# Dividing the attention weights on ScalarE ahead of VectorE's transpose, with the values matmul five steps behind

## The chip, the core and the metric

The kernel runs on one core of a Trainium2 chip. A core has five engines, each with its own in-order instruction queue: TensorE (PE in the profile; PEld is its weight load), VectorE (DVE), ScalarE (ACT), GpSimd (POOL) and SyncE (SP), which here issues nearly all DMAs. The metric is the device time of one execution in microseconds; lower is better.

## The reference, cut to what matters

Eight batches of eight heads, 576 rows of 64 numbers each, all fp32. Each row of scores keeps its 32 largest, is turned into weights by exponentials and a division by their sum, and multiplies V; the heads side by side make `x` (4608 by 512), which goes through two matrix multiplications with `h - tanh(h)` between.

```python
scores = scale * np.matmul(q, k.transpose(0, 1, 3, 2))
kth = np.partition(scores, -top_k, axis=-1)[..., -top_k:-top_k + 1]     # top_k = 32
scores = np.where(scores >= kth, scores, -1000000000.0)
attn = np.exp(scores - np.max(scores, axis=-1, keepdims=True))
attn = attn / (np.sum(attn, axis=-1, keepdims=True) + 1e-09)
x = np.matmul(attn, v)                    # then (B,H,S,D) -> (B*S, H*D)
h = x @ w_in                              # 512 -> 2048
out = (h - np.tanh(h)) @ w_out            # 2048 -> 512
```

## The kernel before

**Steps.** The attention is cut into 144 steps. A step is one batch, one pair of heads (`hp`) and one tile of 128 query rows; the two heads of the pair are the index `t`. Batch 0 has 18 steps of one kind (`pe` steps, whose weights TensorE transposes); the other seven batches have 18 steps each, 126 together, whose weights VectorE transposes. Two steps of the same head pair and adjacent query tiles form a pair (`nq = 2`, `i = 0, 1`); the 64 rows left over from two head pairs form a single step (`rem`). Each batch after the first has eight pairs and two such singles.

**What one step does, engine by engine.** `scores` multiplies Q and K on PE into one PSUM tile `scps` (there is only one) and ACT copies it to `sc` (L246). `search` on DVE reads both (L268, L269: min and max of the two halves), then finds the 32 largest in four rounds of MAX8 (L276) and MATCH_REPLACE8 (L279). `mask` makes a threshold on POOL (`tb`, L295), a relu on ACT (L308, one instruction per head), a subtraction on POOL (L311) and a check on POOL (`bad`, L315), which reads the search's work tile `ab` (two of these exist). `expo` takes exponentials on ACT with their sums (L331) and POOL adds a small number to the sums (`rd`, L341). `invert` takes the reciprocal on DVE, once for a pair (L346). `turn_z` transposes the weights in 32 by 32 blocks on DVE into `zx` (L377); there are two `zx` places. `spread_keys` sends `zx` to DRAM (`there`, L390) and back in another order (`et`, L392, four DMAs); there is one `et` place for pairs and one, `et_rem`, for singles. `values` multiplies V with `et` on PE (L436) into `av`.

**Division before.** The weights stay undivided. `spread` copies the reciprocals out to 64 columns on POOL (`rx`, L356), PE transposes that (L444) beside `av`, ACT copies both to `xs` (L448), and POOL multiplies the two into `xT` (L460; L451 for singles).

**The feed-forward part.** Each finished unit of 128 or 256 rows of `x` puts its items into a work list: H items (`ffn_h`, L489, PE; after every second one ACT takes `tanh` and a copy, L501 and L502, and POOL subtracts, L503) and O items (`ffn_o`, L510, PE; after eight of them ACT copies the result, L520, and SP stores it). H and O results share two PSUM tiles.

**Order.** The order of every engine's queue is the order in which the Python loop emits. Iteration `n` emits: `values` of the step that is `lag` behind; `mask(n - 1)`; `search(n)`, in whose round 0 the function `between` puts `invert(n - 2)` and `turn_z(n - 2)`; `spread_keys(n - 2)` if that step closes a pair; then feed-forward items, `scores(n + 1)`, items, `expo(n - 1)`, items, and the loads of K, Q and V rows. `deal` takes the items from the list at a rate that `rate` sets so that the list lasts until the next unit is due. `lag` is 2 for `pe` steps and 4 for the others. V rows of a head pair are loaded one iteration before its first step.

Of the kernel before, what the change touches and what calls it, by code (L numbers as in the profile page):

```python
# [17 lines left out]
TOP = 32  # L18
EPS = 1.0e-9
J = 4  # L20


class Step:
# [4 lines left out]
    def __init__(self, b, hp, qt, unit, col, i=0, nq=1, pe=False):  # L28
        self.b, self.hp, self.qt, self.unit, self.col = b, hp, qt, unit, col
        self.i, self.nq, self.pe = i, nq, pe  # L30
        self.rem = qt == J
        self.last = i == nq - 1

        self.lag = 2 if pe else 4


class Unit:
# [11 lines left out]
def kernel(  # L49
# [9 lines left out]
    nc = tc.nc  # L59
# [10 lines left out]
    G = 32  # L70
    NG = P // G
    KC = 2 * S // P
    G = 32
    NG = P // G
    WJ = 4
    FJ = CF // WJ
    scale = 1.0 / float(D) ** 0.5
# [5 lines left out]
    def pool(name, bufs, **kw):  # L83
        return ctx.enter_context(tc.tile_pool(name=name, bufs=bufs, **kw))
# [5 lines left out]
    abpool = pool("ab", 2)  # L90
    mpool = pool("m", 3)
    zpool = pool("z", 2)
    etpool = pool("et", 1)
    xpool = pool("x", 2)
    xrpool = pool("xr", 1)
    thpool = pool("th", 4)
# [16 lines left out]

    spare = consts.tile([P, 4, NW, 2], U32, name="spare")
    later = spare[:].rearrange("p a n w -> p (a n w)").bitcast(FP32)
    zx2 = [consts.tile([P, 4 * S], FP32, name="zx")[:], later[:, 0 : 4 * S]]
    et_rem = later[:, 4 * S : 6 * S]
    e1151 = consts.tile([P, 1], FP32, name="e1151")
    nc.gpsimd.memset(e1151[:], 1151.0 * 2.0**23)
# [5 lines left out]

    first = zx2[0][:, 0 : 4 * NW].bitcast(U32).rearrange("p (a n w) -> p a n w", a=2, w=2)
    slots = [(spare[:, i], spare[:, 2 + i], 8 * CD) for i in range(2)]
    slots.append((first[:, 0], first[:, 1], 8 * CD))  # L130
    for j in reversed(range(WJ)):
# [52 lines left out]
    def half(t):  # L184
        return slice(t * D, (t + 1) * D)
# [155 lines left out]
        nc.gpsimd.tensor_scalar(rd[:, g.i, :], den[:], EPS, None, ALU.add)  # L341

    def invert(n):
        if steps[n].last:
            rd = rds[n][:, 0 : steps[n].nq, :]
            nc.vector.reciprocal(rd, rd)  # L346

    rxs = {}

# [7 lines left out]
                rx[:, 0:nq], rd[:, 0:nq].unsqueeze(3).to_broadcast([P, nq, 2, D])  # L357
            )

    zxs, ets, last_zx = {}, {}, [0]  # L360

    def group(a):
        return slice(a * G, (a + 1) * G)
# [6 lines left out]
    def turn_z(n):  # L370


        g, z = steps[n], st.pop(n)["z"]
        if g.i == 0:
            last_zx[0] ^= 1
        zx = zxs[n] = zxs.pop(n - 1) if g.i else zx2[last_zx[0]]
        nc.vector.transpose(  # L377
            tiles(zx, g.nq)[:, :, :, g.i, :].rearrange("p c k j -> p k c j"),
            z[:].rearrange("p (k c j) -> p k c j", c=NG, j=G),
        )  # L380

    def spread_keys(n):


        zx = zxs.pop(n)
        rem = steps[n].rem
        et = ets[n] = et_rem if rem else etpool.tile([P, 4 * S], FP32, tag="et", name="et")
        w = steps[n].nq * S // 2
        there = dpool.tile([P, NG * w], FP32, tag=f"there{steps[n].nq}", name="there")
        nc.sync.dma_start(there[:], zx[:, 0 : NG * w])  # L390
        for c in range(NG):
            nc.sync.dma_start(  # L392
                et[group(c), 0 : NG * w].rearrange("i (a x) -> i a x", a=NG),
                there[:, c * w : (c + 1) * w].rearrange("(a i) x -> i a x", a=NG),
            )

    def turn_pe(n):

        g, z = steps[n], st.pop(n)["z"]
        if g.rem:  # L400
            et = et_rem
        elif g.i:
            et = ets.pop(n - 1)
        else:
            et = etpool.tile([P, 4 * S], FP32, tag="et", name="et")[:]
        ets[n] = et
        et = tiles(et, g.nq)[:, :, :, g.i, :].rearrange("p a k j -> p k a j")
        for k0 in range(0, KC, J):
            kn = min(J, KC - k0)
            zt = zt_ps.tile([P, 512], FP32, tag="zt", name="zt")  # L410
            for k in range(kn):
                nc.tensor.transpose(  # L412
                    zt[:, k * P : (k + 1) * P], z[:, (k0 + k) * P : (k0 + k + 1) * P], ident[:]
                )
            nc.scalar.copy(  # L415
                et[:, k0 : k0 + kn],
                zt[:, 0 : kn * P].rearrange("p (k a j) -> p k a j", a=NG, j=G),
            )
            if k0:
                yield  # L420

    def values(n):

        g = steps[n]
        nq, u = g.nq, g.unit
        et = tiles(ets.pop(n), nq)
        rx = rxs.pop(n)
        w = nq * P
        av = zt_ps.tile([P, 2, N], FP32, tag="zt", name="av")
        for i in range(2 if g.rem else 1):  # L430
            cols = half(i) if g.rem else slice(0, w)
            es = et[:, 2 * i : 2 * i + 2] if g.rem else et
            hp = g.hp + i
            for c in range(J + 1):
                for t in range(2):
                    nc.tensor.matmul(  # L436
                        av[half(t), 0, cols],
                        vb[g.b, hp][:, t, c, :] if c < J else vr[g.b, hp][:, t, :],
                        es[:, :, (J + 1) * t + c if c < J else J].rearrange("p a i j -> p a (i j)"),
                        start=(c == 0),  # L440
                        stop=(c == J),
                    )
        for i in range(nq):
            nc.tensor.transpose(  # L444
                av[:, 1, 0:w].rearrange("p (a i j) -> p i a j", a=NG, i=nq)[:, i], rx[:, i].rearrange("p t d -> p (t d)"), ident[:]
            )
        xs = xrpool.tile([P, 2, N], FP32, tag="xs", name="xs")
        nc.scalar.copy(xs[:, :, 0:w], av[:, :, 0:w])  # L448
        if g.rem:
            for i in range(2):  # L450
                nc.gpsimd.tensor_tensor(  # L451
                    xt(u)[:, g.hp + i, g.col : g.col + R],
                    xs[:, 0, half(i)],
                    xs[:, 1, half(i)],
                    ALU.mult,
                )
        else:

            xv = xs[:, :, 0:w].rearrange("p s (a i j) -> p s i a j", a=NG, i=nq)
            nc.gpsimd.tensor_tensor(  # L460
                xt(u)[:, g.hp, g.col : g.col + w].rearrange("p (i a j) -> p i a j", a=NG, i=nq),
                xv[:, 0],
                xv[:, 1],
                ALU.mult,
            )
        if n in done:
            work.extend(ffn(u))

# [104 lines left out]
    def run(exact):  # L573
# [4 lines left out]
        def at(n, fn):  # L578
            todo.setdefault(n, []).append(fn)
# [3 lines left out]
        for i, (b, hp) in enumerate(pairs):  # L583
            n = next(n for n, g in enumerate(steps) if (g.b, g.hp) == (b, hp))
            for x, name in enumerate("kq"):
                m = max(n - 5 + x, turned.get(name, -4))
                if b == 0 and not exact:
                    m = -4
                at(m, lambda x=(name, b, hp, exact): load_rows(*x))
                if x and i < NHP and not exact:  # L590
                    at(-4, lambda: load_piece())
                turn = lambda x=(name, b, hp): turn_rows(*x)
                if 0 < i < NHP:
                    at_round.setdefault((n - 1, 0), []).append(turn)
                    turned[name] = n - 1
                else:
                    at(n - 3 + x, turn)
                    turned[name] = n - 3 + x
            at(n - 1, lambda b=b, hp=hp: load_v(b, hp))

# [41 lines left out]
        def between(i):  # L644
            for fn in at_round.pop((n, i), []):
                fn()
            if i == 0 and here(-2):
                invert(n - 2)
                if not steps[n - 2].pe:
                    turn_z(n - 2)  # L650


        ready, begun = {}, {}
# [13 lines left out]
        def rate():  # L667


            have, low, high = len(work), 0.0, None  # L670
            coming = sorted((t, u.n // 8) for u, t in ready.items() if t > n)
            for t, k in coming + [(NS + 4, 0)]:
                r = have / max(t - n, 1)
                high = r if high is None else min(high, r)
                have += k
            for u, t in begun.items():
                if t > n and u in before:
                    need = [i + 1 for i, x in enumerate(work) if x[1] is before[u]]
                    if need:
                        low = max(low, need[-1] / (t - n))  # L680
            return max(low, high)
# [8 lines left out]
                credit -= 1  # L690
            credit = min(credit, 1.0)

        for n in range(-4, NS + 4):
            pe = here(-2) and steps[n - 2].pe
            if here(-3) and not steps[n - 3].pe:
                spread(n - 3)
            for m in (n - 4, n - 3):
                if 0 <= m < NS and steps[m].last and steps[m].lag == n - m:
                    values(m)
            share, usable = rate(), converted[0]  # L700
# [5 lines left out]
            if here(0):  # L706
                search(n, exact, between)
            elif here(-2):
                between(0)
            if here(-2) and not pe and steps[n - 2].last:  # L710
                spread_keys(n - 2)
            if pe:
# [63 lines left out]
```

## Time and profile before

| | |
|---|---|
| time, median of 3 runs | 1538.54 us (1538.29 to 1539.8) |
| the profiled execution | 1541.86 us, of which the span of the profile is 1540.1 us |
| PE | 1441.5 us busy, 94% of the span |
| DVE | 1346.9 us busy, 87% |
| POOL | 940.9 us busy, 61% |
| ACT | 883.4 us busy, 57% |
| granted TensorE clock over the span | 0.981 |

A row of groups reads: line, engine, operation, output<-input by the program's names, shapes, count, then busy time in us, mean ns of one instruction, and the engine's idle time just ahead of them with what ended it. A row of the timeline reads: start in us, length in us, engine, line, operation, and in brackets the idle time ahead of it and its releaser. The profile shows two matmul instructions for each fp32 multiplication of the program, and one for a transpose.

### The profile page before, as it was taken

How to read it: one execution, taken by the hardware profiler on the slowest of the kernel's cores; microseconds unless marked ns; L12 is line 12 of the kernel's file. 1: busy time of each engine (PE TensorE's matmuls, PEld its weight loads, DVE VectorE, ACT ScalarE, POOL GpSimd, SP SyncE). 2: the span in 40 equal slices, each digit the busy share in tenths (PEclk: the TensorE clock that was granted, in tenths of full speed). 3: DMA queues.
4: the chain of work that ended last, by engine and by line, in shares of the span. 5: the costliest groups of instructions: out<-in, count | busy, mean ns of one | idle time of the engine just before them, and what ended most of it. 6: DMA issues, size and time to landing. Idle time of an engine off the chain costs nothing.

```text
span 1540.1 us, 24174 instructions
## 1 busy us (share of the span) xinstructions
PE 1441.5 (94%) x7428; PEld 911.6 (59%) x7428; DVE 1346.9 (87%) x3828; ACT 883.4 (57%) x1567; POOL 940.9 (61%) x1525
## 2 busy tenths in 40 slices
PE   2567898999999999999999999999999999999997
PEld 1355566556566665656566665656566665656673
DVE  6988899999999999999999999999999999997300
ACT  4887776556555565556565565656565565655320
POOL 2777677567575675757575675757575675746420
PEclk9887999999999999999999999999999999999999
DMA  9944114546754575446655565456655566534400
GB/s 233 367 168 172 50 32 102 143 130 176 173 157 137 146 168 161 127 141 154 177 136 146 146 161 160 128 149 154 172 136 149 146 153 165 147 114 116 137 7 16
DMA packets 255466, 221.61 MB, mean 144 GB/s; under 512 B 197728, under 2 KB 204896, under 8 KB 248160
## 3 DMA queue, kind: packets, MB, share of 16 engines
q1 hardware_dynamic: 253552, 219.75, 53.1%
q8 instruction: 61, 1.00, 0.3%
q14 instruction: 77, 0.63, 0.2%
q10 hardware_dynamic: 1776, 0.22, 0.1%
HBM read 136.17 MB, written 83.76 MB: 143 GB/s over the span
## 4 chain that ended last, share of the span: by engine, by line
PE 79%; DVE 7%; ACT 4%; DMA 3%; issue 2%; SPq 2%; POOL 2%; DVEq 0%; ACTq 0%; POOLq 0%
PE hps L489 30%; PE ops L510 29%; PE av L436 10%; PE scps L238 9%; DVE m L276 2%; DVE ab L279 2%; PE av L444 2%; SPq L201 1%; DMA et<-there 1%; ACT z L308 1%; ACT f L159 1%; PE zt L412 1%; DMA zx<-in_moe_w_in_dram 1%; DVE ab L268 1%; DVE ab L271 1%
## 5 line engine op out<-in xcount | busy, mean ns | idle before, releaser
L510 PE MATMUL ops<-w_out,g 128*128 128x512 f32 x1152 | 520.5, 598 | 0.0
L489 PE MATMUL hps<-xT,w_in 128*128 128x256 f32 (+1 forms) x2176 | 471.4, 372 | 1.2 <-POOL xT L460 1.2
L276 DVE MAX8 m<-ab 128x8 f32<-128x288 f32 (+1 forms) x1152 | 464.1, 444 | 0.0
L311 POOL TENSOR_TENSOR z<-sc,z 128x576 f32<-128x576 f32 x288 | 400.2, 1412 | 77.1 <-ACT z L308 77.1
L489 PEld LDWEIGHTS hps<-xT,w_in 128*128 128x128 f32 x2176 | 390.7, 193 | 73.9 <-issue 20.7
L279 DVE MATCH_REPLACE8 ab<-m,ab 128x288 f32<-128x288 f32 x864 | 376.0, 443 | 0.0
L510 PEld LDWEIGHTS ops<-w_out,g 128*128 128x128 f32 x1152 | 211.4, 191 | 244.7 <-issue 240.7
L308 ACT ACTIVATE z<-sc,tb 128x576 f32<-128x576 f32 x288 | 207.6, 769 | 153.8 <-POOL tb L295 153.8
L503 POOL TENSOR_TENSOR g<-g,th 128x512 f32<-128x512 f32 x144 | 183.8, 1276 | 123.5 <-ACT g L502 109.0
L331 ACT ACTIVATE z<-z,nb 128x576 f32<-128x576 f32 x288 | 221.6, 773 | 8.7 <-POOL z L311 8.6
L246 ACT COPY sc<-scps 128x1152 f32<-128x1152 f32 x144 | 160.8, 1116 | 108.5 <-PE scps L238 106.4
L238 PE MATMUL scps<-kT,qT 64*128 64x288 f32 (+1 forms) x1280 | 188.1, 445 | 30.2 <-DVE qT L223 27.7
L238 PEld LDWEIGHTS scps<-kT,qT 64*128 64x128 f32 (+1 forms) x1280 | 101.4, 184 | 118.9 <-issue 56.4
L436 PE MATMUL av<-et,vb 128*64 128x256 f32 (+1 forms) x1088 | 133.3, 381 | 38.4 <-ACT et L415 30.6
L268 DVE TENSOR_TENSOR ab<-scps,sc 128x576 f32<-128x576 f32 x144 | 107.6, 747 | 68.0 <-POOL bad L315 55.0
L460 POOL TENSOR_TENSOR xT<-xs 128x256 f32<-128x256 f32 (+1 forms) x68 | 47.2, 695 | 168.0 <-ACT xs L448 168.0
L501 ACT ACTIVATE th<-hps 128x512 f32<-128x512 f32 x144 | 85.4, 593 | 106.8 <-PE hps L489 104.4
L448 ACT COPY xs<-av 128x512 f32<-128x512 f32 (+1 forms) x84 | 44.1, 525 | 169.6 <-PE av L444 169.6
L436 PEld LDWEIGHTS av<-et,vb 128*64 128x64 f32 x1088 | 75.2, 140 | 101.0 <-issue 36.3
L341 POOL TENSOR_SCALAR rd<-den 128x2 f32<-128x2 f32 x144 | 33.4, 232 | 139.4 <-ACT z L331 90.9
L271 DVE MAX8 ab<-ab 128x8 f32<-128x288 f32 x288 | 116.5, 446 | 0.0
L269 DVE TENSOR_TENSOR ab<-scps,sc 128x576 f32<-128x576 f32 x144 | 107.5, 747 | 0.0
(67 smaller groups left out, 1249.5 us busy)
## 6 DMA issues: line engine op xcount, KB each, us to landing
et<-there SPq DMA_DIRECT2D x224, 288.0 KB, 5.3
there<-spare SPq DMA_DIRECT2D x28, 1152.0 KB, 4.2
there<-zx SPq DMA_DIRECT2D x28, 1152.0 KB, 4.2
kin<-in_k_dram SPq DMA_DIRECT2D x116, 72.0 KB, 2.4
vb<-in_v_dram SPq DMA_DIRECT2D x64, 128.0 KB, 4.5
out_dram<-ot SPq DMA_DIRECT2D x32, 256.0 KB, 3.3
qin<-in_q_dram SPq DMA_DIRECT2D x113, 72.0 KB, 3.4
spare<-there SPq DMA_DIRECT2D x56, 144.0 KB, 3.0
```

Source lines behind the costliest of these rows:

```text
L238: nc.tensor.matmul(ps[rows, t, s, 0:S2], qT[g.b, g.hp + i][half(t), qs], kT[g.b, g.hp + i][half(t), ks], start=True, stop=True,)
L246: nc.scalar.copy(sc[:], ps[:, :, :, 0:S2])
L271: nc.vector.max(ab[:, t, S2 : S2 + 8], lo[:, t, :])
L276: nc.vector.max(m[:, t, m8], last[t] if i == rounds - 1 else cur[t])
L279: nc.vector.match_replace(nxt[t], m[:, t, m8], cur[t], NEG)
L308: nc.scalar.activation(zv[:, t, :], scf[:, t, :], AF.Relu, bias=tb[:, t : t + 1], scale=-BIG)
L311: nc.gpsimd.tensor_tensor(zv[:, t, :], scf[:, t, :], zv[:, t, :], ALU.subtract)
L331: nc.scalar.activation(x["zv"][:, t, :], x["zv"][:, t, :], AF.Exp, bias=x["nb"][:, t : t + 1], scale=scale, accum_out=den[:, t : t + 1],)
L436: nc.tensor.matmul(av[half(t), 0, cols], vb[g.b, hp][:, t, c, :] if c < J else vr[g.b, hp][:, t, :], es[:, :, (J + 1) * t + c if c < J els ...
L489: nc.tensor.matmul(cur[u][:, s : s + w], w_in[j][:, c, fo : fo + P], u.xT[:, c, 0:w], start=(c == 0), stop=(c == CD - 1),)
L503: nc.gpsimd.tensor_tensor(g, g, th[:], ALU.subtract)
L510: nc.tensor.matmul(cur[u][:], u.g[o // 1024][:, o % 1024 // 512, o % 512 : o % 512 + P], w_out[f // FJ][:, f % FJ, :], start=(f == 0), sto ...
```

## The change

On the 126 steps that are not `pe` steps:

- `invert` takes the reciprocal of every step, not once for a pair, still in round 0 of `search(n)`.
- A new function `divide` follows it: ACT multiplies the weights in place by the reciprocals, one instruction per head.
- `turn_z` is emitted after round 3 of `search(n)` (`LATE`) instead of in round 0.
- `spread`, the transposes of `rx`, and POOL's multiplication are gone; ACT copies `av` straight into `xT`.
- `lag` is 5 instead of 4; the loop and `rate` reckon with one iteration more.
- There is one `zx` place instead of two, and two `et` places for pairs instead of one.
- V rows are loaded one iteration after the head pair's first step (batch 0: as before).

`pe` steps keep their way.

```diff
+LAG = 5
-        self.lag = 2 if pe else 4
+        self.lag = 2 if pe else LAG
...
+    LATE = 3
-    zx2 = [consts.tile([P, 4 * S], FP32, name="zx")[:], later[:, 0 : 4 * S]]
+    zx1 = consts.tile([P, 4 * S], FP32, name="zx")[:]
+    et2 = [consts.tile([P, 4 * S], FP32, name="et")[:], later[:, 0 : 4 * S]]
...
     def invert(n):
-        if steps[n].last:
-            rd = rds[n][:, 0 : steps[n].nq, :]
+        g = steps[n]
+        if g.last and g.pe:
+            rd = rds[n][:, 0 : g.nq, :]
             nc.vector.reciprocal(rd, rd)
+        elif not g.pe:
+            rd = rds[n]
+            nc.vector.reciprocal(rd[:, g.i, :], rd[:, g.i, :])
+
+    def divide(n):
+
+        g = steps[n]
+        for t in range(2):
+            x = st[n]["zv"][:, t, :]
+            nc.scalar.activation(x, x, AF.Copy, scale=rds[n][:, g.i, t : t + 1])
+        if g.last:
+            rds.pop(n)
...
-        if g.i == 0:
-            last_zx[0] ^= 1
-        zx = zxs[n] = zxs.pop(n - 1) if g.i else zx2[last_zx[0]]
+        zx = zxs[n] = zx1
...
-        et = ets[n] = et_rem if rem else etpool.tile([P, 4 * S], FP32, tag="et", name="et")
+        if not rem:
+            last_et[0] ^= 1
+        et = ets[n] = et_rem if rem else et2[last_et[0]]
...
-        for i in range(nq):
-            nc.tensor.transpose(
-                av[:, 1, 0:w].rearrange("p (a i j) -> p i a j", a=NG, i=nq)[:, i], rx[:, i].rearrange("p t d -> p (t d)"), ident[:]
-            )
-        xs = xrpool.tile([P, 2, N], FP32, tag="xs", name="xs")
-        nc.scalar.copy(xs[:, :, 0:w], av[:, :, 0:w])
+        if g.pe:
+            rx = rxs.pop(n)
+            for i in range(nq):
+                nc.tensor.transpose(
+                    in_order(av[:, 1, 0:w], nq)[:, i], rx[:, i].rearrange("p t d -> p (t d)"), ident[:]
+                )
+            xs = xrpool.tile([P, 2, N], FP32, tag="xs", name="xs")
+            nc.scalar.copy(xs[:, :, 0:w], av[:, :, 0:w])
+
+        def put(dst, order, cols):
+            if g.pe:
+                nc.gpsimd.tensor_tensor(dst, order(xs[:, 0, cols]), order(xs[:, 1, cols]), ALU.mult)
+            else:
+                nc.scalar.copy(dst, order(av[:, 0, cols]))
...
-            at(n - 1, lambda b=b, hp=hp: load_v(b, hp))
+            at(n + 1 if b else n - 1, lambda b=b, hp=hp: load_v(b, hp))
...
                 invert(n - 2)
                 if not steps[n - 2].pe:
-                    turn_z(n - 2)
+                    divide(n - 2)
+            if i == LATE and here(-2) and not steps[n - 2].pe:
+                turn_z(n - 2)
...
-            for t, k in coming + [(NS + 4, 0)]:
+            for t, k in coming + [(NS + LAG, 0)]:
...
-        for n in range(-4, NS + 4):
+        for n in range(-4, NS + LAG):
-            if here(-3) and not steps[n - 3].pe:
-                spread(n - 3)
-            for m in (n - 4, n - 3):
+            for m in (n - LAG, n - LAG + 1, n - LAG + 2):
```

More of the change, by code (lines that the diff above doesn't have):

```diff
@@ L72 @@
     KC = 2 * S // P
-    G = 32
-    NG = P // G
+    LATE = 3
     WJ = 4
@@ L92 @@
     zpool = pool("z", 2)
-    etpool = pool("et", 1)
     xpool = pool("x", 2)
@@ L124, in flat @@
         return x.rearrange("p n w -> p (n w)")
-    first = zx2[0][:, 0 : 4 * NW].bitcast(U32).rearrange("p (a n w) -> p a n w", a=2, w=2)
+    first = zx1[:, 0 : 4 * NW].bitcast(U32).rearrange("p (a n w) -> p a n w", a=2, w=2)
     slots = [(spare[:, i], spare[:, 2 + i], 8 * CD) for i in range(2)]
@@ L358, in spread @@
             )
-    zxs, ets, last_zx = {}, {}, [0]
+    zxs, ets, last_et = {}, {}, [0]
     def group(a):
@@ L404, in turn_pe @@
         else:
-            et = etpool.tile([P, 4 * S], FP32, tag="et", name="et")[:]
+            et = et2[0]
         ets[n] = et
@@ L420, in turn_pe, with in_order @@
                 yield
+    def in_order(x, nq):
+        return x.rearrange("p (a i j) -> p i a j", a=NG, i=nq)
     def values(n):
@@ L426, in values @@
         et = tiles(ets.pop(n), nq)
-        rx = rxs.pop(n)
         w = nq * P
@@ L442, in values @@
                     )
-        for i in range(nq):
-            nc.tensor.transpose(
-                av[:, 1, 0:w].rearrange("p (a i j) -> p i a j", a=NG, i=nq)[:, i], rx[:, i].rearrange("p t d -> p (t d)"), ident[:]
-            )
-        xs = xrpool.tile([P, 2, N], FP32, tag="xs", name="xs")
-        nc.scalar.copy(xs[:, :, 0:w], av[:, :, 0:w])
+        if g.pe:
[11 more added lines that the diff above has]
+                nc.scalar.copy(dst, order(av[:, 0, cols]))
         if g.rem:
             for i in range(2):
[L451 to L456, printed above, removed]
-        else:
[L459 to L465, printed above, removed]
+                put(xt(u)[:, g.hp + i, g.col : g.col + R], lambda x: x, half(i))
+        else:
+            dst = xt(u)[:, g.hp, g.col : g.col + w].rearrange("p (i a j) -> p i a j", a=NG, i=nq)
+            put(dst, lambda x: in_order(x, nq), slice(0, w))
         if n in done:
@@ L709, in run @@
                 between(0)
+                between(LATE)
             if here(-2) and not pe and steps[n - 2].last:
```

## The prediction

> **What bounds the kernel now.** I read the engine shares first, then busy time by stretch, PE's waits, PE's timeline, and last the rows of what is added and removed.
>
> ```profile
> PE 1441.5 (94%) x7428; PEld 911.6 (59%) x7428; DVE 1346.9 (87%) x3828; ACT 883.4 (57%) x1567; POOL 940.9 (61%) x1525
> ```
> ```profile
> core 0: us, PE busy (x) PEld busy (x) DVE busy (x) ACT busy (x) POOL busy (x), PEclk, DMA share, GB/s
> 260.00:407.00 147.00, 138.09 (x657) 79.97 (x657) 145.31 (x417) 83.57 (x148) 93.43 (x159) 0.99 0.61 157
> 407.00:1427.00 1020.00, 1019.10 (x5224) 637.53 (x5221) 960.63 (x2727) 586.72 (x1033) 651.73 (x1077) 1.00 0.57 148
> ```
> There are two stages. Up to about 407 us DVE is full (145.3 of 147) and PE is not: DVE sets the pace, and PE has too little feed-forward work. From 407 us PE is full (1019.1 of 1020) and DVE waits 6% of the time. The waits of 410 to 1530 us, PE's and then DVE's:
>
> ```profile
> PE hps L489 <- POOL xT L460: 1.0, 5, 0.2
> DVE ab L268 <- POOL bad L315: 47.7, 52, 4.4
> DVE ab L268 <- ACT sc L246: 11.0, 9, 2.8
> ```
> PE waits 1.0 us in all there, so everything after is PE work laid end to end. DVE's waits are on POOL and ACT work that itself stands behind PE results in those queues. PE's timeline where the stages meet, and one wait ahead of it:
>
> ```profile
> 270.60 3.40 PE L436 MATMUL av<-et,vb 128*64 128x256 f32 x16 [3.48 <-DMA et<-there]
> ...
> 399.57 1.24 PE L238 MATMUL scps<-kT,qT 64*128 64x288 f32 x8
> 405.43 1.95 PE L436 MATMUL av<-et,vb 128*64 128x256 f32 x16 [0.99 <-issue]
> 407.74 0.44 PE L444 MATMUL av<-ident,rx 128*128 128x128 f32 x2
> 408.01 1.46 PE L489 MATMUL hps<-xT,w_in 128*128 128x256 f32 x6
> ...
> 434.97 1.95 PE L436 MATMUL av<-et,vb 128*64 128x256 f32 x16
> 441.11 1.24 PE L238 MATMUL scps<-kT,qT 64*128 64x288 f32 x8
> ```
> The last idle time of note ends at 405.43. Read starts, not lengths: two transposes of `rx` start at 407.74 and the next multiplication at 408.01, so they cost 0.27 us, though the row says 0.44.
>
> By the Trainium skill ("Perfetto Trace Analysis", Identifying the Most-Contended Engine) matmul busy time is a bad measure, and weight-load busy is to be taken. That is 637.5 of 1020, 63%, and speaks against this change: DVE (94%) would be the bound, taking work from PE worth nothing, and the added reciprocals a loss of 4.7 us. But DVE waits 58.7 us in this stage and PE 1.0, which decides for PE.
>
> **The change part by part.**
>
> *PE.* The `rx` transposes of 56 pairs and 14 singles go. From start to start a pair's take 0.274 us and a single's 0.166 us: 56 x 0.274 + 14 x 0.166 = 17.7 us. The skill ("TensorE: Matmul & The Clock Gate", PE-mode transpose) gives some 275 ns for one in a kernel; 126 of them would be 34.7 us. The trace's starts decide. Only what goes behind the DVE-paced stage counts.
>
> *The fifth step of lag.* A unit's feed-forward items come one step later. In the emitted order of PE's instructions, the items emitted ahead of `scores(42)` (the one at 441.11) come to 195.3 us before and 186.3 us after, at the timeline's pitches (H 0.448 us, O 0.875 us a multiplication). So 9.0 us leave the DVE-paced stage, where PE has room, for the stage where it has none. This is the change's cost on PE.
>
> *Where PE takes over.* PE work from `scores(42)` to the end, by the same pitches (scores 1.17, values of a pair 2.31): 1091.6 us before, 1088.6 us after, so -3.0: 9.0 us of items in, the transposes of the PE-paced stage and some timing of values out. The same sum from `scores(38)` at 399.57 ends 2 us past the traced end, so it can be trusted. But PE also reaches `scores(42)` earlier. Before it was already behind, at 441.1. After, with less to do, it is held only by DVE: `scores(42)` needs `scps` free, which is 1.5 us (L268, L269) into `search(41)`, and that starts at 434.6. The work of the two steps before, 10.3 and 8.3 us from the same limit at 417.3, ends at 436.0 too. So PE starts the rest at 436.2: -4.9. Together **-7.9 us**.
>
> *DVE.* 126 reciprocals instead of 70, at 0.084 us from start to start (row mean 168 ns, overlapped): +4.7 us, about 12 of the 56 ahead of `scores(42)`, +1.0 us. Against that, the 3.48 us wait of PE for `et` at 270.60, which ends in a 1.7 us stall of DVE on POOL at 280.8, should go, because the values come a step later. I call the two even. After 442 us DVE needs about 164 us for 18 steps and PE 170, so DVE keeps up. `turn_z` now waits for `divide`; behind it on DVE stands only the next `search`, which waits anyway for the `sc` copy that follows `divide` on ACT.
>
> *ACT.* This is the new load.
>
> ```profile
> L308 ACT ACTIVATE z<-sc,tb 128x576 f32<-128x576 f32 x288 | 207.6, 769 | 153.8 <-POOL tb L295 153.8
> L448 ACT COPY xs<-av 128x512 f32<-128x512 f32 x60 | 35.2, 586 | 149.0 <-PE av L444 149.0
> L460 POOL TENSOR_TENSOR xT<-xs 128x256 f32<-128x256 f32 x60 | 43.6, 727 | 165.6 <-ACT xs L448 165.6
> ```
> The trace has no `divide`. L308 has its shape and also one per-partition operand: 769 ns, or 1.36 us for two from start to start. Below, half of the 1152-wide copy L246 is 0.56 us each; above, an exponential with its sum is 0.97 us. I take L308. 252 of them add 194 us; the narrower copy of `av` (373 ns for 128x256 in L448's other form) gives 11 back. ACT goes from 57% to about 69%.
>
> The cost lies in the queue order. `divide(n - 2)` waits for the reciprocal, about 4 us into `search(n)`, and behind it on ACT stand `sc(n + 1)`, which DVE waits for, and tanh with copy, which frees PE's two PSUM tiles. But `relu(n - 1)`, ahead of it, starts earlier than now: POOL's multiplication of `xT` no longer stands ahead of `tb`, and the `av` copy is shorter. That returns about 1.1 us in steps with values. Tight are the steps with H items, whose order is now: `sc`, exponentials, twice tanh and copy, (POOL subtract, `tb`), relu, `divide`, next `sc`.
>
> ```profile
> 1391.49 1.12 ACT L246 COPY sc<-scps 128x1152 f32<-128x1152 f32 x1
> 1398.24 1.44 ACT L308 ACTIVATE z<-sc,tb 128x576 f32<-128x576 f32 x2 [2.03 <-POOL tb L295]
> 1399.59 0.57 ACT L501 ACTIVATE th<-hps 128x512 f32<-128x512 f32 x1
> 1402.57 0.78 ACT L331 ACTIVATE z<-z,nb 128x576 f32<-128x576 f32 x1
> ```
> From start to start: `sc` 1.02, exponentials 1.53, tanh and copy 2 x 1.05, POOL subtract 1.28, first `tb` 0.34, relu 1.36, `divide` 1.36, handoffs about 0.3: a ring of 9.3 us. PE needs (8.30 + 10.48)/2 = 9.4 us a step after the change. It fits, barely. I add 1 us for places where it doesn't.
>
> *POOL and SP.* POOL loses `rx` (26 us) and the multiplications (50 us): worth nothing by itself, as POOL is not full, beyond the order above. The DRAM trip (`there` and four `et` DMAs) starts up to 3.4 us later in the step, and SP's stores and K, Q and V loads behind it too. Hidden: K and Q land two steps ahead of use, V loaded at `n + 1` is used at `n + 6`, and values have one step (9.4 us) more against 3.4. With one `zx`, the next pair's first transpose must find `there` read out: 4.2 us to landing against a whole step. If that cover went, DVE would wait a few us a pair.
>
> **Sum.** -7.9 + 1 = about -7 us, against the profiled execution's span of 1540.1 and its 1541.86 us, itself 0.2% above the median. Applied to the median of 1538.54: **1531.5 us**.
>
> **The rivals.**
>
> - *B: the gain is eaten in the DVE-paced stage.* ACT holds `sc` back a little there and `search(41)` starts 3 to 5 us late, so PE's head start is lost and only -3.0 remains. For it: DVE has no slack there (145.3 of 147). Against: ACT is 57% busy there. Time about 1537.
> - *C: ACT's ring becomes the bound, and it is slower.* If `divide` is nearer an exponential (0.97 us) or handoffs are longer, the ring passes 9.4 us in H steps; then tanh comes late, PE waits for `hps` and DVE for `sc`. About 50 H steps follow `scores(42)`. An excess of 0.3 us costs 15 us: about 1546. It decides from an excess of 0.16 us, where 50 steps eat 8 us. For it: one queue now holds both engines. Against: steps with values make ACT wait for PE, so lateness does not add up from step to step.
> - *D: PE is not the bound, by weight loads.* Then only the reciprocals show: +4.7, about 1543.
> - *E: the division does not hide but serialises DVE* (`turn_z` waiting each step). That would be C seen on DVE; I count it there.
>
> **How the numbers follow.** About 0.2%, 3 us, is what a measurement of this kernel can tell from no change. A 0.62, B 0.15, C 0.18, D 0.05. A is faster whole, and a quarter of B is (under 1535.5); the rest of B is the same; C and D are slower, save a sliver of each within 3 us. A's own range is 1526 to 1536. To leave no more than 2 in 10 out, the range takes in B, D and the near part of C: 1525 to 1546. Faster 0.65, same 0.13, slower 0.22.
>
> **What would show it.** Right: no L444 past batch 0; PE's last wait for `et` gone; PE's `scores` near 436 us instead of 441.11; PE waiting for under 3 us after that; L357 (`divide`) near 769 ns; DVE's waits on POOL `bad` shorter, those on ACT `sc` longer. Wrong: PE waits on ACT (`g`, or `xT`) in H steps add up to 8 us or more (C); DVE waits on `divide` or `sc` ahead of 430 us (B); steps after 450 us whose length follows DVE instead of PE (D).

## The result, and the profile after

| | before | after |
|---|---|---|
| time, median | 1539.17 us (1538.29 to 1540.68, 4 runs) | 1534.32 us (1533.38 to 1534.82, 4 runs) |
| the profiled execution | 1541.86 us, span 1540.1 us | 1534.82 us, span 1533.0 us |
| granted TensorE clock over the span | 0.981 | 0.979 |

The ratio is 0.9967, with a 95% interval of 0.9949 to 0.9984: the changed kernel is 5.1 us faster (2.5 to 7.8). The same kernel was run again beside the later experiments (e7) and gave 0.9965 (0.9953 to 0.9978). The prediction said 1531.5 us, 7 us less than before; its sign was right, its size a little large.

The profile's line of busy times after the change:

```profile
PE 1432.2 (93%) x7302; PEld 901.9 (59%) x7302; DVE 1349.9 (88%) x3884; ACT 1021.6 (67%) x1833; POOL 871.3 (57%) x1371
```

PE has 126 instructions fewer (the transposes) and is 9.3 us less busy; ACT has gone from 57% to 67%. The two stages by stretch:

```profile
core 0: us, PE busy (x) PEld busy (x) DVE busy (x) ACT busy (x) POOL busy (x), PEclk, DMA share, GB/s
260.00:407.00 147.00, 135.75 (x628) 78.49 (x628) 147.00 (x427) 103.04 (x182) 87.66 (x145) 0.98 0.61 159
407.00:1427.00 1020.00, 1019.14 (x5161) 633.25 (x5160) 969.50 (x2795) 706.42 (x1268) 596.07 (x955) 1.00 0.57 150
```

In the first stage DVE is now full to the hundredth (147.00 of 147): still the bound. In the second PE is still at 1019.14 of 1020. The waits from 410 to 1530 us, PE's first, then DVE's:

```profile
PE scps L238 <- DVE ab L269: 0.4, 1, 0.4
PE hps L504 <- ACT g L517: 0.4, 1, 0.4
```
```profile
DVE zx L388 <- ACT z L357: 42.5, 37, 6.2
...
DVE ab L268 <- ACT sc L246: 5.2, 4, 1.6
DVE ab L268 <- POOL bad L315: 0.2, 1, 0.2
```

PE again waits for nothing of note: 0.8 us. DVE's 47.7 us of waits on `bad` have gone, and 42.5 us on the division have come; with those on `sc` its 58.7 us are now 47.9, time that DVE has to spare because PE sets the pace. Where PE takes over:

```profile
405.95 1.24 PE L238 MATMUL scps<-kT,qT 64*128 64x288 f32 x8 [1.64 <-DVE ab L269]
...
415.44 1.24 PE L238 MATMUL scps<-kT,qT 64*128 64x288 f32 x8 [0.38 <-DVE ab L269]
...
432.21 1.99 PE L504 MATMUL hps<-xT,w_in 128*128 128x256 f32 x8 [0.37 <-ACT g L517]
434.31 1.24 PE L238 MATMUL scps<-kT,qT 64*128 64x288 f32 x8
```

The last three waits that the profile lists in the old stage stand in brackets; `scores(42)` is the item at 434.31, against 441.11 before. DVE's last read of `scps` in `search(41)`, before and after:

```profile
436.30 0.74 DVE L269 TENSOR_TENSOR ab<-scps,sc 128x576 f32<-128x576 f32 x1
```
```profile
433.50 0.76 DVE L269 TENSOR_TENSOR ab<-scps,sc 128x576 f32<-128x576 f32 x1
```

Before, `scores(42)` starts 4.07 us after that read has ended, after the change 0.05 us. The same 0.05 us stands in e1, e3, e6 and e7: there DVE releases it, though the profile lists no wait. By its own work PE would have been there 0.18 us earlier: the last H instruction starts 0.49 us ahead of `scores(42)`, where 0.31 is usual. The rows of the division and of the transpose behind it:

```profile
L357 ACT ACTIVATE z<-z,rd 128x576 f32<-128x576 f32 x252 | 180.3, 763 | 44.3 <-DVE rd L350 44.3
L388 DVE STREAM_TRANSPOSE zx<-z 128x1152 f32<-128x1152 f32 x126 | 172.6, 1370 | 42.8 <-ACT z L357 42.5
```

**Where the 7.1 us between the two profiled spans are.** I cut each span at two instructions: the start of `search(16)` (L268) on DVE, up to which PE's instructions stand in the same order in all kernels of this text, and `scores(42)` on PE. The cut at `search(16)` is needed because that first stretch varies by itself: the two profiles of the changed kernel (here and e7) have it at 207.4 and 204.5 us.

| us | before | after | difference |
|---|---|---|---|
| start to `search(16)` | 209.0 | 207.4 | -1.6 |
| `search(16)` to `scores(42)` | 232.1 | 226.9 | -5.2 |
| `scores(42)` to PE's end | 1090.4 | 1090.5 | +0.1 |
| PE's end to the span's end | 8.6 | 8.2 | -0.4 |

The head start is there, the saving in PE's own work behind it is not. The stretch from `scores(42)` on, split from start to start of PE's instructions by kind (e1 and e3 are explained below):

| us from `scores(42)` on | before | after | e1: fifth step only | e3: after + a dummy transpose |
|---|---|---|---|---|
| scores | 118.9 | 118.9 | 118.9 | 119.0 |
| H items | 406.8 (2064 instr.) | 416.9 (2104) | 415.7 (2104) | 413.9 (2104) |
| O items | 424.6 (959) | 427.3 (959) | 424.2 (959) | 424.2 (959) |
| values | 124.4 | 126.6 | 126.7 | 126.7 |
| transposes | 14.9 | 0 | 15.2 | 9.9 |

Look at the O items: the same 959 instructions take 2.7 us longer after the change than before, though PE waits for nothing. That is what the experiments had to explain.

### The profile page after: what moved, and what is told of

Read it like the earlier page. It is cut to its first block, busy times and chain, and to the rows that moved or that the text cites. A ratio compares the mean times of both kernels' runs of the same rounds, so it can differ in the third digit from the quotient of the medians.

```text
span 1533.0 us, 24064 instructions
## 1 busy us (share of the span) xinstructions
PE 1432.2 (93%) x7302; PEld 901.9 (59%) x7302; DVE 1349.9 (88%) x3884; ACT 1021.6 (67%) x1833; POOL 871.3 (57%) x1371
## 4 chain that ended last, share of the span: by engine, by line
PE 75%; DVE 13%; ACT 5%; SPq 2%; DMA 2%; POOL 1%; issue 1%; DVEq 0%; ACTq 0%; POOLq 0%
PE ops L525 29%; PE hps L504 28%; PE av L453 9%; PE scps L238 8%; DVE m L276 3%; DVE ab L279 3%; DVE zx L388 2%; SPq L201 1%; DVE ab L269 1%; DVE ab L271 1%; DVE ab L268 1%; DMA zx<-in_moe_w_in_dram 1%; PE zt L425 1%; ACT z L308 1%; ACT sc L246 1%
## 5 line engine op out<-in xcount | busy, mean ns | idle before, releaser
L311 POOL TENSOR_TENSOR z<-sc,z 128x576 f32<-128x576 f32 x288 | 401.0, 1415 | 209.0 <-ACT z L308 209.0
L308 ACT ACTIVATE z<-sc,tb 128x576 f32<-128x576 f32 x288 | 207.6, 769 | 89.7 <-POOL tb L295 78.2
L388 DVE STREAM_TRANSPOSE zx<-z 128x1152 f32<-128x1152 f32 x126 | 172.6, 1370 | 42.8 <-ACT z L357 42.5
L357 ACT ACTIVATE z<-z,rd 128x576 f32<-128x576 f32 x252 | 180.3, 763 | 44.3 <-DVE rd L350 44.3
L246 ACT COPY sc<-scps 128x1152 f32<-128x1152 f32 x144 | 159.2, 1105 | 11.3 <-PE scps L238 10.2
L268 DVE TENSOR_TENSOR ab<-scps,sc 128x576 f32<-128x576 f32 x144 | 105.7, 734 | 13.9 <-ACT sc L246 6.5
L453 PE MATMUL av<-et,vb 128*64 128x256 f32 (+1 forms) x640 | 77.2, 373 | 30.4 <-ACT et L428 30.4
L535 ACT COPY ot<-ops 128x512 f32<-128x512 f32 x36 | 21.0, 584 | 114.3 <-PE ops L525 114.3
```

Source lines behind the costliest of these rows:

```text
L308: nc.scalar.activation(zv[:, t, :], scf[:, t, :], AF.Relu, bias=tb[:, t : t + 1], scale=-BIG)
L311: nc.gpsimd.tensor_tensor(zv[:, t, :], scf[:, t, :], zv[:, t, :], ALU.subtract)
L357: nc.scalar.activation(x, x, AF.Copy, scale=rds[n][:, g.i, t : t + 1])
L388: nc.vector.transpose(tiles(zx, g.nq)[:, :, :, g.i, :].rearrange("p c k j -> p k c j"), z[:].rearrange("p (k c j) -> p k c j", c=NG, j=G),)
L453: nc.tensor.matmul(av[half(t), 0, cols], vb[g.b, hp][:, t, c, :] if c < J else vr[g.b, hp][:, t, :], es[:, :, (J + 1) * t + c if c < J els ...
```

## The experiments

All ratios are to the kernel before, run beside it on the same chip; "against the change" is the difference of two such ratios (times 1540 us), with 0.9967 for the change, or 0.9965 where e7 ran on the same chip. The change's own interval is 2.6 us each way, those of the experiments 1.4 to 2.3, so differences of some 3 us (e3, e6) lie at the edge of what the times can tell; there the profiles decide.

**e1: the fifth step alone.** The kernel before, with `lag` 5, the places for `zx` and `et` and the later V loads of the change, but the division as before (`rx` transposed on PE, multiplied on POOL) and `turn_z` in round 0. Theory: the prediction's account of PE's time ("ledger" in the expectations). Rival: the step of lag is itself the gain.

```diff
-        self.lag = 2 if pe else 4
+        self.lag = 2 if pe else 5
...
-            at(n - 1, lambda b=b, hp=hp: load_v(b, hp))
+            at(n + 1 if b else n - 1, lambda b=b, hp=hp: load_v(b, hp))
...
-            for m in (n - 4, n - 3):
+            for m in (n - 5, n - 4, n - 3):
```

> The fifth step of lag, with its places for et and zx and the later V loads, but with the division as before (rx, its transposes, POOL's multiplication, transpose of the weights in round 0). Theory 'ledger' (PE time after the takeover decides): 9.0 us of feed-forward items move behind the takeover and PE gets some 5 to 7 us of head start for it, with nothing taken from PE: 0 to +4 us against before (1539 to 1543). Rival 'lag pays' (the gain of the change is the waits for et that the fifth step removes): -3 to -5 us, as the whole change.

Measured: 1544.9 us, ratio 1.0031 (1.0021 to 1.004): 4.8 us slower, a little above the theory's 1539 to 1543. The rival falls. The head start is there as with the whole change (-5.8 us to `scores(42)`, from `search(16)`), so it comes from the fifth step, not from the division. What follows grows by 11.1 us: in the table, +8.9 for 40 more H instructions and +2.3 for one more pair's values. The prediction had 9.0 for the items. Division on ScalarE on top of this is then worth 1.0031 to 0.9967, about -10 us.

**e2: the division at four steps.** The changed kernel with `LAG = 4`.

```diff
-LAG = 5
+LAG = 4
...
-            for m in (n - LAG, n - LAG + 1, n - LAG + 2):
+            for m in (n - LAG, n - LAG + 1):
```

> The changed kernel with the values four steps behind instead of five. Theory 'ledger': the 9.0 us of items go back into the stage where PE has room, PE is again behind at the takeover, and only the transposes are saved: -7 to -9 us against before, so 2 to 4 us faster than the change (1530 to 1532). Rival 'lag pays': with turn_z at the end of the step the et DMAs land too late for lag 4, PE waits for et in the later stage as well, and it is no faster than before, or slower (1538 to 1560).

Measured: 1570.0 us, ratio 1.019 (1.0176 to 1.0204), beyond both. PE's waits from 410 to 1530 us in this kernel:

```profile
PE av L453 <- DMA spare<-there: 14.9, 15, 2.0
PE av L453 <- DMA et<-there: 13.9, 15, 2.2
PE av L453 <- issue: 0.8, 2, 0.6
```

Thirty of the values wait about 1 us each for the return from DRAM; before, at the same lag, none did past 410 us. From `search(16)` on, 10.8 us are lost against before ahead of `scores(42)`, where values wait for the return too, and 21.6 us behind it. That the late transpose is the reason is argued, not isolated: the division and the single `zx` place come with it. So the fifth step, a loss by itself, is what the change needs: without it the trip through DRAM has no cover.

**e3: one transpose back.** The changed kernel, with one 128x128 identity transpose behind the values of each unit, whose result nobody reads. By then the trace suggested a cost of changing between full 128*128 multiplications (H and O) and narrower ones (scores 64*128, values 128*64). Compare how O items return after values, before the change:

```profile
455.94 0.60 PE L436 MATMUL av<-et,vr 128*64 128x256 f32 x4
456.47 0.44 PE L444 MATMUL av<-ident,rx 128*128 128x128 f32 x2
456.75 3.60 PE L510 MATMUL ops<-w_out,g 128*128 128x512 f32 x8
460.28 1.24 PE L238 MATMUL scps<-kT,qT 64*128 64x288 f32 x8
```

and after it:

```profile
461.65 0.60 PE L453 MATMUL av<-et,vr 128*64 128x256 f32 x4
462.19 1.98 PE L525 MATMUL ops<-w_out,g 128*128 128x512 f32 x4
464.10 1.24 PE L238 MATMUL scps<-kT,qT 64*128 64x288 f32 x8
```

An undisturbed O instruction takes 0.429 us from start to start. Before: eight take 460.28 - 456.75 = 3.53, that is 8 x 0.429 + 0.10: something is lost once, ahead of `scores`. After: four take 464.10 - 462.19 = 1.91, that is 4 x 0.429 + 0.19: it is lost twice. Instruction by instruction, 0.094 us go at the start of a narrow group and 0.104 us at the second full-width instruction after it. A transpose behind the values is 128*128 itself, and the 0.104 us does not appear behind it. From 440 to 1520 us both kernels return 161 times from narrow to full width; 59 of these returns had a transpose behind them before, so 102 paid the 0.104 us, and after the change all 161 do.

The return is not the only place where it appears. Where PE has waited inside a run of H instructions, with no narrow group near, the second instruction behind the wait is late by the same 0.104 us: five times before (behind the waits for `xT`), once after (432.21 above), 31 of 31 times in all the traces here from 405 us on.

```diff
+        else:
+            nc.tensor.transpose(av[:, 1, 0:P], ident[:], ident[:])
```

> The changed kernel with one 128x128 transpose of the identity behind the values of each pair and each single (70 more; its output goes to the unused half of av and is not read). Theory 'switch': without transposes PE pays 104 ns in the second multiplication after it comes back from the 64-column tiles of values to full tiles, and a transpose takes that on itself. One transpose (0.166 us) then costs only 0.06 us net: 70 x 0.06 = +4 us against the change, and the 104 ns are gone from the starts behind values. Rival 'no switch': the 104 ns have another cause, stay, and 70 x 0.166 = +11.6 us is paid (slower than before by some 7 us).

Measured: 1538.22 us, ratio 0.9987 (0.9977 to 0.9996), about 3.1 us against the change; PE's work from `scores(42)` on grew by 3.8 us. The theory had 4, the rival 11.6. The same place in this kernel:

```profile
461.49 0.60 PE L453 MATMUL av<-et,vr 128*64 128x256 f32 x4
462.02 0.33 PE L469 MATMUL av<-ident 128*128 128x128 f32 x1
462.19 1.88 PE L527 MATMUL ops<-w_out,g 128*128 128x512 f32 x4
464.00 1.24 PE L238 MATMUL scps<-kT,qT 64*128 64x288 f32 x8
```

The four O instructions are back to 1.81 us. In the table, 60 dummy transposes cost 9.9 us and give back 3.1 in O and 3.0 in H. So a single transpose of 0.166 us is worth 0.06 net and a pair's 0.274 us is worth 0.17.

**e4: more work in ScalarE's ring.** One more pass over half the weights on ACT, in place, behind the division of each of the 126 steps.

```diff
+            if t:
+                nc.scalar.activation(x, x, AF.Copy, scale=1.0)
```

> The changed kernel with one more ScalarE pass over half the weights of a step, a copy in place behind the second division (126 more, 0.6 to 0.7 us each). Theory 'ring nearly full': ScalarE's ring of 9.3 us in H steps goes to 9.9 to 10.0 us against the 9.4 us that PE needs, and some 50 H steps lose 0.5 us each: +15 to +30 us against the change (1550 to 1565). Rival 'ring has room': lateness is taken back where ScalarE waits for values, and it costs under 5 us (under 1539).

Measured: 1540.71 us, ratio 1.0004 (0.9995 to 1.0014), about 5.7 us against the change: between the two expectations, nearer the rival. 82 us more of ACT work cost 6. PE's waits from 410 to 1530 us add up to 4.6:

```profile
PE ops L527 <- issue: 1.5, 3, 0.5
PE ops L527 <- POOL rd L341: 1.4, 2, 0.7
PE hps L506 <- ACT g L519: 1.3, 1, 1.3
PE scps L238 <- DVE ab L269: 0.4, 1, 0.4
```

ACT's own waits from 440 to 1420 us show who paid. In the changed kernel and then here:

```profile
ACT xT L473 <- PE av L453: 81.0, 45, 4.8
ACT ot L535 <- PE ops L525: 66.6, 25, 2.7
ACT th L516 <- PE hps L504: 57.4, 41, 2.0
```
```profile
ACT xT L475 <- PE av L455: 66.6, 34, 4.1
ACT ot L537 <- PE ops L527: 42.7, 25, 2.5
ACT th L518 <- PE hps L506: 25.9, 27, 1.8
```

These three sum to 205.0 and 135.2 us: ACT had spent that time waiting for PE, and 70 of the 82 us came out of it. The ring was not full. The 4.6 us of PE's waits and the 5.7 us of the time belong together: PE's work from `scores(42)` on is 5.5 us longer.

**e5, e8, e9: fewer switches.** If each return costs 0.104 us and each start of a narrow group 0.094, then values placed right behind `scores` save both for every unit. e5 moves them there (`LAG = 4`: late in iteration m + 4 of the loop instead of at the start of m + 5, so that the return from DRAM has almost as much time as in the change); items and their order stay.

```diff
-LAG = 5
+LAG = 4
...
-                    ready[g.unit] = m + g.lag + g.pe
+                    ready[g.unit] = m + g.lag + 1
...
-        for n in range(-4, NS + LAG):
+        for n in range(-4, NS + LAG + 1):
-            for m in (n - LAG, n - LAG + 1, n - LAG + 2):
-                if 0 <= m < NS and steps[m].last and steps[m].lag == n - m:
-                    values(m)
...
             if here(-1):
                 expo(n - 1)
+            for m in (n - LAG, n - LAG + 1):
+                if 0 <= m < NS and steps[m].last and steps[m].lag == n - m:
+                    values(m)
```

> The changed kernel with values moved from the start of iteration m + 5 to iteration m + 4 right behind scores and expo, so that on TensorE the 64-column tiles of values follow those of scores. The feed-forward items keep their places in the order. Theory 'switch': each excursion from full tiles to the narrower ones costs 94 ns going and 104 ns coming back, and 62 excursions behind the takeover (49 pairs, 13 singles) fall away: -10 to -12 us against the change (1523 to 1525). Rival 'no switch': the order of the same work on TensorE does not matter, within 2 us of the change; or the et DMAs land too late for it, as with lag 4, and it is slower.

Measured: 1542.89 us, ratio 1.002 (1.0011 to 1.0029), about 8 us slower than the change. Both were wrong. Of the change's 322 losses of 0.094 or 0.104 us (161 starts and 161 returns) from 440 to 1520 us 114 are gone, some 11 us, as meant (the 77 in e8's expectation counts PE's new waits among those left), but PE has a new wait. Its waits from 440 to 1530 us:

```profile
PE hps L504 <- ACT g L517: 8.2, 10, 0.8
PE ops L525 <- POOL rd L341: 4.3, 5, 0.9
PE ops L525 <- issue: 1.9, 3, 0.6
```

That is 14.4 us where the change has none, and read from start to start the new waits hold PE up by 19 us: PE's work from `scores(42)` on is 8.0 us longer, with 11 saved. An example: two tanh-and-copy pairs stand back to back on ACT behind the exponentials (450.43 to 452.45 us in this trace), and with no values between the items any more PE reaches the next H or O before its PSUM tile is free. The first of the two copies ends at 451.47 and PE's O starts at 451.57, after 0.86 us of waiting. All 18 waits end like this, 0.10 us behind such a copy for O and 0.05 us for H, also where the profile names POOL or "issue". e8 and e9 only move the shares of items that a step deals out: ahead of `scores`, behind the values, and in the two places after. e5 has 0.4, 0.2, 0.2, 0.2.

```diff
-            deal(0.0 if pe else 0.4)
+            deal(0.0 if pe else 0.6)
...
-            deal(0.0 if pe else 0.2)
+            deal(0.0 if pe else 0.1)
...
-            deal(0.2)
+            deal(0.2 if pe else 0.1)
```

This is e8: 0.6, 0.2, 0.1, 0.1. e9 has 0.2, 0.3, 0.3, 0.2.

> As e5 (values right behind scores and the exponentials), but the shares of feed-forward items dealt out around them in a step are 0.6 ahead of scores and 0.1 in the two places behind the values, instead of 0.4, 0.2, 0.2. e5 kept the saving of some 77 switches of 0.104 us between full and narrow tiles, but lost about 16 us to some 20 waits of TensorE on ScalarE's copies and on the feed-forward tiles. Theory 'order': those waits come of where the tanh and copy instructions fall in ScalarE's queue; with more items ahead of scores most of them go, and the time is 8 to 12 us below e5, 1525 to 1531, ratio 0.990 to 0.995. Rival 'capacity': ScalarE's queue has no room behind the values in whatever order: the waits stay and the ratio is 1.000 or above.

Measured: 1521.19 us, ratio 0.9881 (0.9866 to 0.9896): the fastest of all, 18 us faster than before and 13 faster than the change, and below the theory's 1525 to 1531. The rival, that ACT has no room behind the values in whatever order, falls. From 440 to 1530 us the profile lists no wait of PE at all. `scores`, values and O items now stand like this:

```profile
449.54 3.17 PE L525 MATMUL ops<-w_out,g 128*128 128x512 f32 x7
452.64 1.24 PE L238 MATMUL scps<-kT,qT 64*128 64x288 f32 x8
453.92 1.95 PE L453 MATMUL av<-et,vb 128*64 128x256 f32 x16
455.67 0.63 PE L453 MATMUL av<-et,vr 128*64 128x256 f32 x4
456.23 7.13 PE L525 MATMUL ops<-w_out,g 128*128 128x512 f32 x16
```

One start and one return for scores and values together. Counted from 440 to 1520 us, 104 starts and 104 returns are left of 161 each after the change: 114 fewer, 11.3 us less. From `scores(42)` to PE's end this kernel takes 1077.6 us, 12.9 less than the change, of which 1.7 are eight H instructions that fall ahead of the cut.

> As e8, with the shares moved the other way: 0.2 ahead of scores, 0.3 and 0.3 in the two places behind the values, 0.2 last. Theory 'order': more items behind the values puts more tanh and copy instructions behind the exponentials and ahead of the division; the waits of TensorE grow against e5's 16 us, and the ratio is 1.004 or above (1546 us or more). Rival 'capacity': the shares do not matter, and the ratio is within 0.002 of e5's 1.002.

Measured: 1539.61 us, ratio 0.9998 (0.9989 to 1.0007). The direction expected was wrong: it is not slower than e5. The waits on the feed-forward tiles are gone here too, and another took their place. PE's waits from 440 to 1530 us:

```profile
PE scps L238 <- DVE ab L269: 7.1, 16, 0.8
PE scps L238 <- ACT g L517: 4.2, 5, 0.9
PE av L453 <- issue: 0.4, 2, 0.2
```

With few items ahead of `scores`, PE reaches it before DVE and ACT have read the one `scps` tile out. So the number of switches is cut in all three; of the three, only the shares of e8 keep every tile free in time.

**e6: the transpose two rounds earlier.** The changed kernel with `LATE = 1`.

```diff
-    LATE = 3
+    LATE = 1
```

> The changed kernel with the transpose of the weights after round 1 of the search instead of after round 3 (LATE = 1). Theory: the reciprocal ends round 0, round 1 takes some 1.8 us, and the two divisions take 1.5 us plus handoffs, so VectorE would wait for them in most steps, by some 0.5 us where ScalarE is on time and by 2 us and more where ScalarE is late; in the VectorE-paced stage of 18 steps that delays the takeover by 5 to 15 us, and behind it the spare time of VectorE (about 6 us in 18 steps) is used up in H steps: +5 to +25 us against the change. Rival: the place of the transpose does not matter, as VectorE has time to wait: within 2 us.

Measured: 1537.74 us, ratio 0.9984 (0.9975 to 0.9993), about 2.9 us slower than the change: the sign of the theory, a fraction of its size. DVE waits for the division 50.6 us instead of 42.5 from 410 to 1530 us, most of which PE's pace hides. Ahead of that, where DVE sets the pace, `search(41)` starts 2.3 us later (227.7 us after `search(16)` against 225.4); the stretch behind `scores(42)` is 1.8 us longer.

**e7: the changed kernel again,** beside e5 and e6.

> The changed kernel as it is, on the same chip as the other two: 0.995 to 0.998 of before.

Measured: 1534.52 us, ratio 0.9965 (0.9953 to 0.9978). PE's work from `scores(42)` on took 1090.5 us, as in the first profile, although `search(16)` came at 204.5 us instead of 207.4.

## Why the prediction was right, and where it was off

- **PE is the bound, not DVE (rival D): right.** Taking 15 us of transposes away, or putting 10 back (e3), moved the time with PE's sum from start to start. The rule of the Trainium skill that was weighed ("Perfetto Trace Analysis", Identifying the Most-Contended Engine) judges PE by its weight-load busy, one of two measures named there. By it PE at 59% of the span and DVE at 87% would have made DVE the bound, and the change a loss; the 1.0 us that PE waits in 1120 us before (0.8 after) decides against it.
- **The head start: the mechanism right, its size near for two errors that nearly cancel (-5.2 us against -4.9).** Before, PE was late by its own work; after, `scores(42)` starts as soon as `search(41)` has read `scps`, and PE's own work would have ended 0.18 us earlier, so both limits that the prediction named meet, as it said. But it put the start of `search(41)` at 434.6, which is where the last instruction of the search before it starts; L268 stands at 435.66 in the trace of before. Read so, the limit is 437.1 and the head start 4.0 us. The other 1.2 us are DVE's stage, shorter from `search(16)` to `search(41)` (226.6 to 225.4 us), where reciprocals and the vanished `et` stall were called even. In e1, without the added reciprocals, it is 1.8 us shorter, against the 1.7 of the stall.
- **The fifth step's price: about right.** 9.0 us of items were predicted, 8.9 measured in e1 and in the change. The values were named among what leaves this stage; they come in, +2.2 us.
- **The step that failed: the transposes at their starts, 0.274 us a pair and 0.166 a single.** PE's work from `scores(42)` on was to shrink by 3.0 us and grew by 0.1. The transposes took 14.9 us there and are gone; but 59 returns from narrow to full multiplications, whose loss they had absorbed, now cost 0.104 us each, 6.1 us. Against that, four waits of before for `xT` are gone, which held PE up by 1.9 us with the late instruction behind each. In the table: -14.9 transposes, +8.9 items, +2.2 values, +2.7 in O and +1.2 in H (the returns less the waits) is +0.1. From the prediction's -3.0: +6.1 for the returns, -1.9 for the waits, and -0.8 because transposes, items and values come to -3.8, make +0.4; 0.3 stays unassigned.
- **The total is nearer than its parts, which is luck.** -7 was forecast and -5.1 measured: PE's work behind the takeover gave nothing of its 3 us, while the 1 us added for friction was not needed and DVE's stage gave 1.2 us that nobody had counted. What the change gains is the head start; the transposes that it removes, less the returns and with the waits for `xT`, give 10.7 us, about what the items and values of the fifth step take (11.1).
- **The ring on ACT (rival C): the mechanism exists, its threshold was too low.** The division took 763 ns against the 769 taken from L308. A ring of 9.3 us in a step of 9.4 was to decide the result from 0.16 us of excess; e4 added 0.65 us a step and cost 0.05 us a step. The sum was of instructions in H steps taken as a closed loop, while ACT still waited 205 us for PE over all steps. Where the order bunches ACT's work (e5) it does hold PE up. The 1 us of friction in the sum was not there: PE waits 0.4 us for ACT.
- **B, the gain eaten ahead of the takeover: not seen** in the change (DVE waits for nothing from 200 to 430 us in its trace). e6 shows what it looks like: 2.3 us.
- **What would show it.** The waits of DVE on `sc`, said to grow, shrank from 11.0 to 5.2 us; its new waits are at the transpose, on the division. The trip through DRAM was hidden at five steps, as costed (no wait for `et` is left past 200 us), and not at four (e2).

## What to carry to other kernels

Cost a removed instruction by what its neighbours take without it, not by its own length: read both neighbours' starts, here the first and second multiplication behind it. On a PE that waits for nothing, count the changes between full and narrow multiplications and put the narrow groups next to each other; here (e8) that was worth more than the change itself (13 us against 5), but only once the items around them were dealt so that no PSUM tile came late. An engine in a ring with its own waits may have room that a sum over one step hides: sum its waits before calling the ring full, and look where the order bunches its work.

## What was not expected of the hardware

- Between 128*128 multiplications and 64*128 or 128*64 ones, about 0.094 us go on the way to the narrow ones and 0.104 us at the second instruction on the way back (fp32, at a granted clock of 1.00 in this stage), without any wait in the profile. A 128*128 transpose in between takes the second away (e3), and with fewer such changes the loss goes (e8). The shape of the multiplication is not the whole cause: the same 0.104 us stands at the second H instruction behind a wait of PE, 31 of 31 times. What in TensorE makes it stays open.
- An instruction can be held up without a wait in the profile: `scores(42)` came 0.18 us late by its starts, 0.05 us behind the end of DVE's read, in a row without a bracket.
- The stretch ahead of `search(16)`, in which PE's instructions stand in the same order in all kernels here, differs by up to 4.5 us between profiled executions (204.5 to 209.0 us in the three of before and of the changed kernel, 2.9 us of it between two of the same kernel): single profiles are compared from a common instruction on, not from the span's start.
